# Two tiny reads ahead of the weight loads, and a DRAM copy cut into seven pieces, in a layernorm + S5 + SwiGLU kernel

## The chip, the cores and the metric

One core of a Trainium2 chip. The metric is the device time of one execution in microseconds, median of several runs. In the profile PE is TensorE's matmuls, PEld its weight loads, DVE VectorE, ACT ScalarE, POOL GpSimd and SP SyncE, which here only issues transfers. A q behind an engine's name means its instruction queue.

## What is computed

The input x is 2048 rows of 512, in bf16. It is normalised row by row, and the output is x plus an S5 state-space layer of the normalised rows plus a SwiGLU feed-forward layer of them. Cut to what matters:

```python
xn = (x - mean(x)) / sqrt(var(x) + 1e-5)                 # 2048 x 512
# A: S5 with 512 complex states
Bu = xn @ B_bar.T                                        # B_bar from Lambda, log_dt, B
h[t] = Lam_bar * h[t - 1] + Bu[t]
a = 2 * real(h @ C.T) + xn * Dskip
# B: SwiGLU
b = (silu(xn @ w_gate) * (xn @ w_up)) @ w_down           # 512 -> 1376 -> 512
out = x + a + b
```

w_gate and w_up are 512 x 1376 in bf16, so one row is 2,752 bytes and one matrix 1.4 MB.

## The kernel before

The 2048 rows are worked in four chunks of 512 (CW), each of four tiles of 128 rows (TPC); there are NT = 16 tiles. The inner size of 512 is four slices of 128, k = 0 to 3 (KD). The 1376 columns of gate and up are three groups (`fgroups`: columns 0 to 511, 512 to 1023, 1024 to 1279) and a rest of 96, loaded apart (`load_last`). The order of all work on every engine is written out by hand; an engine does its instructions in the order in which the program issues them.

**The head.** The first chunk is begun before any statistics are there. SyncE loads x tile 0 (L124) and ScalarE's queue x tile 1 (L127). Then the four k slices of gate group 0 are loaded in the loop at L129 and L130, through `load_w1_half` (L118): k = 0 and 2 from SyncE, k = 1 and 3 from ScalarE. SyncE goes on with x tile 2 (L131), the two halves of up group 0 (L132 and L133, again L118), x tile 3 (L134), groups 1 and 2 of gate and up (`load_w1`, L113), x tiles 4 to 7 (L143) and the transposing load of B's real part (L147). GpSimd loads three short rows of parameters (L142).

TensorE transposes x tiles 0 and 1 while taking the mean off (L251 and L259), DVE and ACT copy the result to SBUF (L263), and TensorE multiplies it with gate and up (`head_mm`, which calls `sw_mm`, L495): first gate with x tile 0, k = 0 to 3, then gate with x tile 1, then up with x tile 0, k = 0 to 3. Then comes the transpose of x tile 2, for which ACT takes the mean (L234) and DVE centres (L241); up with x tile 1; gate with x tile 2; the transpose of x tile 3; up with x tile 2; gate and up with x tile 3. The factor 1/std is put in when the products are taken out of PSUM (L504, L505). Groups 1 and 2 of the first chunk follow in the same way.

**The rest.** From about 24 us the chunks alternate: products with B (L393), with gate and up (L468), with w_down (L580) and with C (L590). DVE does the complex rotations and the scans (L435), ACT takes products out of PSUM.

**The output.** The output rows of tiles 0 to 11 start as a copy of x from DRAM to DRAM (L826), one transfer of 1.5 MB from SyncE, issued between the products with B of chunk 2 and the output of chunk 0. To it GpSimd's transfers add the results tile by tile (L597) and the skip term chunk by chunk (L564). Tiles 12 to 15 are written whole (L594).

Of the kernel before, what the change touches and what calls it, by code (L numbers as in the profile page):

```python
# [11 lines left out]
BF16 = mybir.dt.bfloat16  # L12
# [11 lines left out]
def kernel(  # L24
# [17 lines left out]
    nc = tc.nc  # L42
    _, L, D = A_x.shape
# [5 lines left out]
    NT = L // 128  # L49
    NCH = L // CW  # L50
    TPC = CW // 128
# [12 lines left out]
    const = ctx.enter_context(tc.tile_pool(name="const", bufs=1))  # L64
# [51 lines left out]
    def load_w1_half(q, tiles, view, gi, k0, k1):  # L116
        a, b = fgroups[gi]
        q.dma_start(out=tiles[gi][:, k0:k1, :], in_=view[:, k0:k1, a * 128:min(F, b * 128)])  # L118
# [7 lines left out]
    nc.vector.memset(minus_mean[:], -1.0 / D)  # L126
    nc.scalar.dma_start(out=xall[:, 1, :], in_=x_v[:, 1, :])  # L127
    nc.scalar.preload_act_table_set("silu_and_others")
    for k in range(KD):  # L129
        load_w1_half(nc.scalar if k % 2 else nc.sync, wg_g, wg_v, 0, k, k + 1)  # L130
    nc.sync.dma_start(out=xall[:, 2, :], in_=x_v[:, 2, :])  # L131
    load_w1_half(nc.sync, wu_g, wu_v, 0, 0, HK)  # L132
    load_w1_half(nc.sync, wu_g, wu_v, 0, HK, KD)  # L133
# [623 lines left out]
    def bproj_chunk(c):  # L757
        need(f"ln{c}")
        for part in range(2):
            for q in range(NQ):  # L760
                bproj_tile(c, part, q)
                pump(BP)
                multiply(0 if q else 1)
# [27 lines left out]
    def queue_ssm(c):  # L791
        fwd, back = ssm_ops(c)
        queue(f"ssm{c}", fwd + back)
# [29 lines left out]
    gateup_chunk(1)  # L823
    nc.gpsimd.dma_start(out=dsk_bc[:], in_=A_Dskip.partition_broadcast(128))
    bproj_chunk(2)
    nc.sync.dma_start(out=out[0, 0:(NT - TPC) * 128, :], in_=A_x[0, 0:(NT - TPC) * 128, :])  # L826
    queue_ssm(2)
    out_chunk(0)
    gateup_chunk(2)
# [45 lines left out]
```

## Time and profile before

| | |
|---|---|
| median of 3 runs | 179.22 us (179.06 to 179.39) |
| the profiled execution | 179.8 us |
| its span | 177.8 us |
| granted TensorE clock | 1.0 |
| DMA, mean over the span | 98 GB/s, 17.36 MB |

The span is the time from the first to the last instruction of the program in the profile; the execution's time has the start and the end around it as well. A group's line has the engine, the operation, output and inputs by the program's names, shapes and count. In a timeline line the first number is the start and the second the time from start to end of the merged instructions, in us; in brackets stands the idle time of the engine before it and what ended it. In a windows line stand, for each engine in the order PE, PEld, DVE, ACT, POOL, the busy time and the number of instructions, then the granted clock, the mean busy share of the 16 DMA engines and the GB/s that they moved. In a waits line the numbers are the total, the times and the longest wait, in us.

### The profile page before, as it was taken

How to read it: one execution, taken by the hardware profiler on the slowest of the kernel's cores; microseconds unless marked ns; L12 is line 12 of the kernel's file. 1: busy time of each engine (PE TensorE's matmuls, PEld its weight loads, DVE VectorE, ACT ScalarE, POOL GpSimd, SP SyncE). 2: the span in 40 equal slices, each digit the busy share in tenths (PEclk: the TensorE clock that was granted, in tenths of full speed). 3: DMA queues.
4: the chain of work that ended last, by engine and by line, in shares of the span. 5: the costliest groups of instructions: out<-in, count | busy, mean ns of one | idle time of the engine just before them, and what ended most of it. 6: DMA issues, size and time to landing. Idle time of an engine off the chain costs nothing.

```text
span 177.8 us, 2376 instructions
## 1 busy us (share of the span) xinstructions
PE 172.8 (97%) x856; PEld 82.5 (46%) x872; DVE 158.2 (89%) x261; ACT 109.0 (61%) x188; POOL 26.7 (15%) x36
## 2 busy tenths in 40 slices
PE   8899999999999999999999999999999999999993
PEld 5354664444444444444444444444444444444743
DVE  3799999999999999999999999999999997799033
ACT  4359989999977678036896661024866658863000
POOL 5162300050000000046000000025000002506100
PEclk9999999999999999999999999999999999999999
DMA  5999969999995000027123000008300001993612
GB/s 154 325 320 222 169 116 246 278 255 194 188 295 177 0 4 0 0 29 72 18 51 71 0 0 0 0 0 84 37 0 2 0 0 8 157 188 35 87 44 77
DMA packets 35115, 17.36 MB, mean 98 GB/s; under 512 B 24960, under 2 KB 35040, under 8 KB 35072
## 3 DMA queue, kind: packets, MB, share of 16 engines
q1 hardware_dynamic: 30928, 13.44, 32.6%
q0 software_dynamic: 3456, 3.28, 14.8%
q10 hardware_dynamic: 720, 0.49, 0.9%
q8 instruction: 7, 0.11, 0.3%
q14 instruction: 4, 0.03, 0.1%
HBM read 8.03 MB, written 5.24 MB: 75 GB/s over the span
## 4 chain that ended last, share of the span: by engine, by line
PE 94%; DMA 3%; issue 1%; SPq 0%; DVE 0%
PE ps L468 29%; PE ps L580 21%; PE ps L393 16%; PE ps L590 15%; PE ps L495 10%; DMA wg<-in_B_w_gate_dram 3%; PE ps L519 2%; PE ps L529 1%; PE ps L251 0%; SPq L118 0%; SPq L124 0%; DVE xall L593 0%; PE ps L287 0%
## 5 line engine op out<-in xcount | busy, mean ns | idle before, releaser
L580 PE MATMUL ps<-wd_sb,guT 128*128 128x512 bf16 (+4 forms) x195 | 38.6, 355 | 0.2
L468 PE MATMUL ps<-xnT,wg 128*128 128x512 bf16 x120 | 30.8, 379 | 0.1
L468 PE MATMUL ps<-xnT,wu 128*128 128x512 bf16 x114 | 30.0, 379 | 0.2
L435 DVE TENSOR_TENSOR_SCAN g<-r_t,car,u 128x512 bf16<-128x512 f32 x24 | 29.0, 1264 | 0.0
L393 PE MATMUL ps<-xnT,BT 128*128 128x512 bf16 x126 | 28.2, 379 | 0.2
L590 PE MATMUL ps<-CF,wt 128*128 128x512 bf16 (+2 forms) x140 | 28.1, 355 | 0.2
L580 PEld LDWEIGHTS <-guT 128*128 128x128 bf16 (+1 forms) x198 | 18.5, 98 | 19.9
L597 POOL DMA_DIRECT2D out_dram<-res x12 | 10.5, 1044 | 83.4 <-ACT res L596 77.5
L596 ACT CAST res<-ps 128x512 bf16<-128x512 f32 x12 | 7.0, 584 | 25.7 <-PE ps L590 23.4
L395 ACT CAST u<-ps 128x512 bf16<-128x512 f32 x32 | 17.9, 593 | 5.6 <-PE ps L393 5.5
L482 ACT ACTIVATE guT<-ps 128x512 bf16<-128x512 f32 x30 | 17.9, 596 | 5.1 <-PE ps L468 5.1
L483 ACT CAST u<-ps 128x512 bf16<-128x512 f32 x30 | 17.6, 586 | 5.1 <-PE ps L468 4.8
L590 PEld LDWEIGHTS <-wt 128*128 128x128 bf16 x144 | 13.5, 98 | 14.3
L393 PEld LDWEIGHTS <-BT 128*128 128x128 bf16 x128 | 12.5, 98 | 14.9
L468 PEld LDWEIGHTS <-wg 128*128 128x128 bf16 x120 | 11.6, 98 | 14.5 <-issue 0.8
L468 PEld LDWEIGHTS <-wu 128*128 128x128 bf16 x120 | 11.7, 98 | 14.2
L552 ACT ACTIVATE xr<-xall,nb,rstd 128x512 bf16<-128x512 bf16 x16 | 11.8, 804 | 4.3 <-DVE xall L560 2.5
L495 PEld LDWEIGHTS <-CF 128*128 128x128 bf16 x96 | 9.3, 99 | 8.9 <-ACT CF L263 1.8
L495 PE MATMUL ps<-wg,CF 128*128 128x512 bf16 (+1 forms) x48 | 11.1, 351 | 0.7 <-DMA wg<-in_B_w_gate_dram 0.7
L204 POOL TENSOR_TENSOR rstd<-ve,neg_half 128x1 f32<-128x1 f32 (+1 forms) x7 | 6.9, 988 | 27.0 <-DVE ve L203 27.0
L495 PE MATMUL ps<-wu,CF 128*128 128x512 bf16 (+1 forms) x47 | 10.6, 343 | 0.1
L194 DVE BATCH_NORM_STATS2 stats<-xall 128x6 f32<-128x512 bf16 x15 | 10.1, 672 | 0.0
(116 smaller groups left out, 200.7 us busy)
## 6 DMA issues: line engine op xcount, KB each, us to landing
out_dram<-in_A_x_dram SPq DMA_DIRECT2D x1, 1536.0 KB, 7.2
out_dram<-res POOLq DMA_DIRECT2D x12, 128.0 KB, 3.2
out_dram<-xall POOLq DMA_DIRECT2D x3, 512.0 KB, 6.6
wd_sb<-in_B_w_down_dram SPq DMA_DIRECT2D x1, 1280.0 KB, 6.8
xall<-in_A_x_dram SPq DMA_DIRECT2D x1, 1024.0 KB, 6.5
wu<-in_B_w_up_dram SPq DMA_DIRECT2D x3, 256.0 KB, 5.3
wg<-in_B_w_gate_dram SPq DMA_DIRECT2D x1, 512.0 KB, 6.1
wu<-in_B_w_up_dram SPq DMA_DIRECT2D x1, 512.0 KB, 4.9
```

Of the source, the lines that this page charges most:

```text
L194: nc.vector.bn_stats(out=stats[:, n, 0, :], in_=xall[:, n, :])
L393: nc.tensor.matmul(ps[:], lhsT=BT[:, part, k, q * 128:(q + 1) * 128], rhs=xnT[:, c, k, :], start=(k == 0), stop=(k == KD - 1))
L395: nc.scalar.copy(out=u_tiles[c][:, part, q, :], in_=ps[:])
L435: V.tensor_tensor_scan(out=g()[:, part, q, :], data0=r_t[:, q:q + 1].to_broadcast([128, CW]), data1=u_tiles[c][:, part, q, :], initial=ini ...
L468: nc.tensor.matmul(ps[:fs, lo:hi], lhsT=wslice(groups, fi, k), rhs=xnT[:, c, k, lo:hi], start=(k == 0), stop=(k == KD - 1))
L482: nc.scalar.activation(out=guT[:fs, fi, :], in_=psg[:fs], func=ACT.Silu)
L483: nc.scalar.copy(out=u_pair[c][:fs, fi % 2, :], in_=psu[:fs])
L495: nc.tensor.matmul(ps[:, 0:(b - a) * 128], lhsT=xcT[:, k, i * 128:(i + 1) * 128], rhs=groups[gi][:, k, :], start=(k == 0), stop=(k == KD - 1))
L552: nc.scalar.activation(out=box["xr"][:], in_=xall[:, n, :], func=ACT.Identity, scale=rstd[:, n:n + 1], bias=nb[:, n:n + 1])
L580: nc.tensor.matmul(o[:], lhsT=gu_tiles[c][:fsz[fi], fi, i * 128:(i + 1) * 128], rhs=wd_sb[:fsz[fi], fi, lo:hi], start=(fi == 0), stop=False)
L590: nc.tensor.matmul(o[:], lhsT=w_tiles[c][:, part, q, i * 128:(i + 1) * 128], rhs=CF[:, part, q, lo:hi], start=False, stop=(part == 1 and q ...
L597: nc.gpsimd.dma_start(out=out_v[:, n, lo:hi], in_=res[:, lo:hi], accum_op=ALU.add)
```

## The change

Two transfers are added on SyncE's queue, `touch(0)` ahead of the gate slices and `touch(1)` between them and x tile 2. Each reads the first two elements (4 bytes) of every 16th row of w_gate or w_up, 32 rows in all, into a small tile `touched` that nothing reads. The copy of x to the output, one transfer of 1536 rows, becomes seven: five of 256 rows and two of 128, one behind the other on the same queue.

```diff
     nc.scalar.preload_act_table_set("silu_and_others")
+    TB = 16
+    touched = const.tile([D // TB, 2, 2], BF16, name="touched")
+
+    def touch(part):
+        src = (B_w_gate, B_w_up)[part].rearrange("(a b) f -> a b f", b=TB)
+        nc.sync.dma_start(out=touched[:, part, :], in_=src[:, 0, 0:2])
+
+    touch(0)
     for k in range(KD):
         load_w1_half(nc.scalar if k % 2 else nc.sync, wg_g, wg_v, 0, k, k + 1)
+    touch(1)
     nc.sync.dma_start(out=xall[:, 2, :], in_=x_v[:, 2, :])
...
     bproj_chunk(2)
-    nc.sync.dma_start(out=out[0, 0:(NT - TPC) * 128, :], in_=A_x[0, 0:(NT - TPC) * 128, :])
+    cuts = [*range(0, NT - TPC - 1, 2), NT - TPC - 1, NT - TPC]
+    for a, b in zip(cuts, cuts[1:]):
+        nc.sync.dma_start(out=out[0, a * 128:b * 128, :], in_=A_x[0, a * 128:b * 128, :])
     queue_ssm(2)
```

## The prediction

> **What bounds the kernel now.** I read the share of busy time first, then the chain of waits, then the waits of TensorE and of the SyncE queue, then the first 12 us instruction by instruction, and last the DMA rate by window. From the page:
>
> ```profile
> PE 172.8 (97%) x856; PEld 82.5 (46%) x872; DVE 158.2 (89%) x261; ACT 109.0 (61%) x188; POOL 26.7 (15%) x36
> ...
> PE 94%; DMA 3%; issue 1%; SPq 0%; DVE 0%
> ```
>
> TensorE (PE) is the chain for 94% of the span; the only other share of weight is a gate load (DMA, 3%). The same chain in order of time, and TensorE's waits with their total:
>
> ```profile
> 1.66 4.99 DMA wg<-in_B_w_gate_dram
> 6.65 0.04 issue
> 6.69 2.36 PE ps L495 x10
> ```
>
> ```profile
> PE ps L647 <- PEq L859: 0.8, 1, 0.8
> PE ps L495 <- DMA wg<-in_B_w_gate_dram: 0.7, 1, 0.7
> ```
>
> After the start TensorE waits once in the whole kernel, for the gate slice k=2, issued by SyncE at 1.66 and landed at 6.65. From 6.69 to the end it runs without a gap, so the end moves by exactly what the stretch before 6.69 gives or takes, as long as no later input comes too late. The stretch itself, TensorE's timeline:
>
> ```profile
> 4.91 0.61 PE L495 MATMUL ps<-wg,CF 128*128 128x512 bf16 x1
> 5.31 0.42 PE L259 MATMUL ps<-diag,minus_mean 128*128 128x256 bf16 x1
> 5.52 0.51 PE L495 MATMUL ps<-wg,CF 128*128 128x512 bf16 x1
> 6.69 1.46 PE L495 MATMUL ps<-wg,CF 128*128 128x512 bf16 x6 [0.66 <-DMA wg<-in_B_w_gate_dram]
> 7.98 1.07 PE L495 MATMUL ps<-wu,CF 128*128 128x512 bf16 x4
> ```
>
> Matmuls of this shape start 0.216 us apart (1.03 us for four, the last one's 0.38 included). Without the wait the third would start at 5.52 + 0.22 = 5.74: the wait is worth 6.69 - 5.74 = 0.95 us. But 7.98 to 9.05 is 0.04 us longer than the other groups of four, because the second half of the up weights (issued 3.13, 5.3 us to landing, so 8.42) comes just when its matmul is due (8.46). Behind the gate slice stands a second bound at the same height: gate alone, made earlier, brings nothing; the up half must come earlier as well.
>
> Why these loads are slow: DMA share and GB/s are the last two columns.
>
> ```profile
> 2.00:3.00 1.00, 1.00 (x7) 0.62 (x5) 0.00 (x0) 0.60 (x1) 1.00 (x2) 1.00 0.98 320
> 3.00:4.00 1.00, 1.00 (x11) 0.80 (x10) 0.82 (x2) 0.53 (x1) 0.55 (x2) 1.00 0.95 238
> 4.00:5.00 1.00, 1.00 (x10) 0.78 (x9) 0.82 (x4) 0.53 (x4) 0.00 (x0) 1.00 0.98 244
> ...
> 7.00:8.00 1.00, 1.00 (x7) 0.41 (x6) 0.12 (x1) 0.72 (x2) 0.18 (x1) 1.00 1.09 386
> ...
> 28.00:29.00 1.00, 1.00 (x6) 0.48 (x5) 0.82 (x2) 1.00 (x3) 0.00 (x0) 1.00 0.61 86
> ...
> 30.00:31.00 1.00, 1.00 (x6) 0.42 (x5) 0.97 (x2) 1.00 (x3) 0.00 (x0) 1.00 1.04 364
> 36.70:37.70 1.00, 1.00 (x6) 0.42 (x5) 1.00 (x2) 1.00 (x3) 1.00 (x1) 1.00 0.86 186
> ...
> 39.70:40.70 1.00, 1.00 (x9) 0.37 (x8) 0.86 (x9) 0.84 (x2) 0.00 (x0) 1.00 1.08 385
> ```
>
> At 3 to 5 us, where the gate slices are read for the first time, 240 GB/s; at 7 to 8 us, where the other columns of the same rows are read, 386. The late x rows (from 27) and the down weights (from 36.7) show the same: slow for some 2 us at the start of a tensor, then full rate. In the packet records a 1,024-byte packet takes 46 ns as a rule, while in 3.0 to 6.6 us single ones take 400 to 1128 ns, and between 6.9 and 8.2 none takes over 180. That looks like a cost of reading a stretch of DRAM for the first time.
>
> **The change, part by part.** *Two touches.* Each is 32 reads of 4 bytes, 16 rows (44 KB) apart, two to each of 16 DMA engines. Issue: a SyncE transfer here takes 0.37 to 0.51 us and POOL's 4-row ones up to 0.71; I take 0.41, the gate slice's own, nearest in queue and kind. The first touch moves gate k=0 from 1.20 to 1.66 and k=2 from 1.66 to 2.12. k=0 landed at 3.80 and is used at 4.91, released by DVE's copy, so 1.1 us cover its delay. k=1 and k=3 go out on ScalarE's queue and don't move. The second touch goes out at about 2.6.
>
> *Waits that shift.* SP's and ACT's transfers take eight semaphores in turn by the trace's records, each issue waiting for the landing of the transfer eight earlier. The waits of SyncE's queue show it once:
>
> ```profile
> SPq L113 <- DMA wg<-in_B_w_gate_dram: 2.1, 1, 2.1
> ```
>
> That is the up load of group 1 waiting until 6.66 for gate k=2 (6.65). With two more transfers in the row x tile 2 must wait for x tile 0 (3.12), the up halves for x tile 1 (3.45) and the first touch, x tile 3 for a gate slice. So x tile 2 goes out at about 3.15 instead of 2.13, the halves at 3.6 and 4.15 instead of 2.60 and 3.13, x tile 3 at 4.6 instead of 3.59: each 1.0 us later. Group 1 of gate waits for gate k=2 in its turn: up to 6.65 instead of 4.10, landing at most about 12.7 instead of 10.18, used at 13.71 (12.76 with the full gain). What follows on that queue (up group 1, group 2, x tiles 4 to 7, the B transposes, the x transpose landing at 20.53 for a use at 24.27) has 1 us or more of cover, so up to about 1 us of delay costs nothing there.
>
> *What the touches may give.* Ahead of the end of the second up half each engine moves 88 packets (x tiles 0 to 2 and four gate slices, 8 each; two halves of 16): 88 x 0.046 = 4.05 us. First packet at 1.76, its first one 0.27 long, about 0.6 from last packet to landing (x tile 0): 1.76 + 0.27 + 4.05 + 0.6 = 6.7 without any long packet, against 8.42 measured. The late issue allows it: 4.15 + 1.0 to the first packet + 16 x 0.046 + 0.6 = 6.5. Full use of the 0.95 us asks for it at 7.46, so half of the long packets' time gone, (8.42 + 6.7) / 2 = 7.6, gives 0.8 us. A second condition: DVE's chain (mean of x tile 2 on ACT, centring, statistics of tile 3, centring at 9.86 to 10.21, used by TensorE at 10.84) begins with x tile 2 at 7.04 and has about 0.5 us to spare; a gain of 0.95 wants x tile 2 by 6.6. Bounds of the part: +0.95 gained if both come early, 0.5 if x tile 2 stays, and, with nothing warmed, up to 1.0 lost (the whole later issue shown in the up half). I take 0.75, between 0.5 and 0.95.
>
> *The copy in seven pieces.* Six more issues of 0.59 us: SyncE busy from 50.84 to about 55.0 instead of 51.4. It has nothing else until the x transpose at 91.33. The copy landed at 58.02, its first reader (the accumulating store) starts at 77.24: 19 us of cover. 2 + 6 is a full turn of eight, so from there on every wait has its old partner. Cost 0; without that cover it would be 6 x 0.59 = 3.5.
>
> *Does the end follow?* DVE is busy without a wait over 0.3 us from 28 to 142, so it cannot follow TensorE forward in that stretch; but its deliveries are early: rotated states of the last chunk done at 161.58 and read from 168.2, the scaled C at 71.74, read at 74.4, where 2.7 us is the least I found. 0.95 fits.
>
> *Sum.* The profiled execution took 179.8 us, of which 177.8 are its span and 2.0 lie around it; 177.8 - 0.75 = 177.05. It was 0.6 us above the median of the runs, 179.22, so I move the median: 179.22 - 0.75 = 178.5.
>
> The page DMA: Bandwidth & Descriptors of the Trainium skill (Latency and other measured facts) puts an HBM access at 0.2 us on average and 2 us at high load. By that rule the long packets come from load, and a touch cures nothing: the time would be 179.2 to 180.2. The trace speaks against it: 386 GB/s at 7 to 8 us with no long packet, 86 GB/s at 28 to 29 with many.
>
> **Rivals.** *The long packets stay and the touches hide* (0.15): they are due to load or rows of 2,752 bytes, or each engine must pay for itself and two rows warm little. The loads land as before, since the slow engine has a backlog: at 4.1 us about 180 of the first 768 packets have not started. For it: some packets of 200 to 750 ns at 8.3 to 10 us, in second reads. Against it: the clean stretch at 7 to 8. Time 179.2, within 0.35.
>
> *SyncE's queue becomes the bound* (0.30, slower): the touches warm too little, and x tile 2, the up halves and x tile 3 start 1.0 us later behind two issues and the shifted waits. It costs from the point where the up half lands after 8.42. For it: that half has 0 spare now. Against it: the backlog covers a part. Half shown: 0.5, whole: 1.0, so 179.7 to 180.2. Under this also falls that first reads are worked off one after the other: then gate gains what up loses.
>
> *The forecast* (0.55): 178.5, its own range 178.2 to 178.8.
>
> A difference under 0.2% (0.36 us) can't be told from no change here. The cases give faster 0.55, same 0.15, slower 0.30. Range: down to 178.1 (0.95 gained, and 0.17 of scatter as in the runs shown), up to 179.9, which leaves out the worse half of the slow case and little below.
>
> **What would show it.** Right: gate k=2 lands by 5.8 and the wait before the third matmul is gone; the second up half by 7.6, x tile 2 by 6.6; 3 to 5 us at over 300 GB/s; long packets few after 3.5 us. Wrong: gate early but TensorE then idle for `wu`, or for x tile 2; the up half after 8.42; the first matmul of L495 later than 4.91 because the touch itself holds up k=0. The copy is wrong if POOL's stores at 77 wait for it.

## The result, and the profile after

The changed kernel takes 179.72 us (median of 22 runs, 179.46 to 181.58), the kernel before 179.22 (22 runs, 178.77 to 179.76): slower, ratio 1.0032, interval 1.0018 to 1.0046, some 0.5 us. The forecast was 178.5. The profiled execution of the changed kernel took 179.73 us, its span is 177.8, the same as in the profile of before. So the two profiles don't show the loss; why is the first thing to be learned here.

New line numbers: L134 issues the touches, L140 loads x tile 2, L143 x tile 3, L504 is `sw_mm` (before L495), L260 and L268 are the transposes (before L251 and L259). The chain of waits of the changed kernel, its first 9 us:

```profile
0.74 2.35 DMA xall<-in_A_x_dram
3.09 0.02 issue
3.11 0.38 SPq L140
...
3.53 0.43 SPq L118
...
4.01 4.37 DMA wu<-in_B_w_up_dram
8.37 0.04 issue
8.42 0.59 PE ps L504 x2
```

Read from below: TensorE waited for the second up half (landed 8.37), which was issued at 4.01, because the first half and x tile 2 (3.11) stood ahead of it on SyncE's queue. In the chain of before the late load was gate k=2. SyncE's timeline:

```profile
0.74 0.39 SPq L124 DMA_DIRECT2D xall<-in_A_x_dram  x1
1.19 0.41 SPq L134 DMA_DIRECT2D touched<-in_B_w_gate_dram  x1
1.65 0.89 SPq L118 DMA_DIRECT2D wg<-in_B_w_gate_dram  x2
2.59 0.43 SPq L134 DMA_DIRECT2D touched<-in_B_w_up_dram  x1
3.11 0.38 SPq L140 DMA_DIRECT2D xall<-in_A_x_dram  x1
3.53 0.94 SPq L118 DMA_DIRECT2D wu<-in_B_w_up_dram  x2
```

In the kernel before, the same stretch of the queue was:

```profile
1.20 0.89 SPq L118 DMA_DIRECT2D wg<-in_B_w_gate_dram  x2
2.13 0.43 SPq L131 DMA_DIRECT2D xall<-in_A_x_dram  x1
2.60 0.95 SPq L118 DMA_DIRECT2D wu<-in_B_w_up_dram  x2
```

A touch costs 0.46 us of the queue (1.19 to 1.65), and x tile 2 and the up halves go out 0.9 to 1.0 us later than before (3.11, 3.53, 4.01 for 2.13, 2.60, 3.13). The turn of the semaphores adds little: SyncE is done with the second touch at 3.02, and x tile 2 waits from there until x tile 0 has landed (3.09). The DMA rate by window (DMA share and GB/s at the end):

```profile
3.00:4.00 1.00, 1.00 (x11) 0.79 (x10) 0.85 (x2) 0.53 (x1) 0.54 (x2) 1.00 0.70 135
4.00:5.00 1.00, 1.00 (x9) 0.75 (x8) 0.81 (x4) 0.56 (x4) 0.00 (x0) 1.00 0.91 285
7.00:8.00 1.00, 1.00 (x6) 0.48 (x5) 0.58 (x2) 0.39 (x2) 0.15 (x1) 1.00 0.90 274
```

No sign of warming: 135 GB/s from 3 to 4 us where it was 238, and 274 at 7 to 8 where it was 386. Between 3 and 8 us the records have 12 packets of 400 ns and more, up to 1032, where the kernel before has 9. The rates alone prove little, because less had been asked for by 4 us; experiments 3 and 7 test it.

**Where the time lies.** In 16 of the 17 profiles of this study, from the first matmul that transposes x tile 2 to the start of the last matmul, 166.00 to 166.01 us pass (166.04 in the other). So a span is the start of that transpose (the *head*), 166.0, 0.55 to the last result of VectorE, and a *tail* from there to the end. The profiles, in us:

| kernel | second up half issued, landed | head | tail |
|---|---|---|---|
| before | 3.13, 8.42 | 8.89 | 2.39 |
| changed | 4.01, 8.37 | 8.85 | 2.39 |
| changed, second profile | 4.00, 8.11 | 8.59 | 2.38 |
| four other profiles with the same loads at the start as before | 3.08 to 3.15, 7.38 to 8.06 | 7.88, 7.94, 8.24, 8.54 | by their transfers, below |

The profile that the forecast was made from has the slowest of five heads of the same code. Its execution, 179.8, was above all the runs known then; the median run has a span near 177.2, so a head near 8.3. In the changed kernel runs from 179.46 to 180.03 stand for heads of 8.5 to 9.1, and two runs (181.04 and 181.58) for something else.

### The profile page after: what moved, and what is told of

The parts are those of the page before. It is cut to its first block, busy times and chain, and to the rows that moved or that the text cites. A ratio compares the mean times of both kernels' runs of the same rounds, so it can differ in the third digit from the quotient of the medians.

```text
span 177.8 us, 2388 instructions
## 1 busy us (share of the span) xinstructions
PE 172.9 (97%) x856; PEld 82.5 (46%) x872; DVE 158.2 (89%) x261; ACT 109.1 (61%) x188; POOL 26.8 (15%) x36
## 4 chain that ended last, share of the span: by engine, by line
PE 93%; DMA 4%; issue 1%; SPq 0%; DVE 0%
PE ps L477 29%; PE ps L589 21%; PE ps L402 16%; PE ps L599 15%; PE ps L504 9%; DMA wu<-in_B_w_up_dram 2%; PE ps L528 2%; DMA xall<-in_A_x_dram 1%; PE ps L538 1%; PE ps L260 0%; SPq L118 0%; SPq L140 0%; DVE xall L602 0%; PE ps L296 0%
## 5 line engine op out<-in xcount | busy, mean ns | idle before, releaser
L504 PEld LDWEIGHTS <-CF 128*128 128x128 bf16 x96 | 9.3, 99 | 8.3 <-issue 0.9
L504 PE MATMUL ps<-wg,CF 128*128 128x512 bf16 (+1 forms) x48 | 10.9, 350 | 0.5 <-DVE CF L272 0.5
L504 PE MATMUL ps<-wu,CF 128*128 128x512 bf16 (+1 forms) x47 | 10.7, 343 | 0.2
```

The costliest lines, as they stand in the source:

```text
L504: nc.tensor.matmul(ps[:, 0:(b - a) * 128], lhsT=xcT[:, k, i * 128:(i + 1) * 128], rhs=groups[gi][:, k, :], start=(k == 0), stop=(k == KD - 1))
```

## The experiments

Theory P: the added transfers only send x tile 2 and the up halves out later, and the touches warm nothing. Rivals: D, the touches' own reads hold up the gate slices; C, the seven pieces cost something; F, the premise of the forecast, that first reads are slow and a touch cures it. The medians differ from session to session, so each stands beside that of before in the same session. Each kernel of the table has 6 to 12 runs. The ratio is taken over all of them and is not that of the two medians, so single long runs raise it (touches_only, gate_touch_8).

| kernel | median | before | ratio (interval) |
|---|---|---|---|
| pieces_only | 179.61 | 179.35 | 1.0014 (1.0000 to 1.0027) |
| touches_only | 180.19 | 179.35 | 1.0068 (1.0040 to 1.0096) |
| x_touches | 180.09 | 179.35 | 1.0043 (1.0030 to 1.0055) |
| pool_touches | 179.67 | 179.35 | 1.0017 (1.0003 to 1.0030) |
| after_again | 179.84 | 179.15 | 1.0041 (1.0025 to 1.0057) |
| x_touches_7 | 179.79 | 179.15 | 1.0033 (1.0021 to 1.0045) |
| late_touches_7 | 179.14 | 179.15 | 0.9997 (0.9980 to 1.0013) |
| tile2_on_act | 179.98 | 179.15 | 1.0042 (1.0025 to 1.0059) |
| copy_3 | 179.66 | 179.38 | 1.0019 (1.0003 to 1.0034) |
| gate_touch_8 | 179.68 | 179.38 | 1.0033 (1.0002 to 1.0064) |
| behind_gate_7 | 179.99 | 179.16 | 1.0040 (1.0026 to 1.0055) |
| up_touch_8 | 179.44 | 179.16 | 1.0011 (0.9998 to 1.0023) |
| after_dummies | 179.89 | 179.16 | 1.0036 (1.0024 to 1.0048) |

**1. The two parts apart.** The kernel before with the seven pieces alone:

```diff
-    nc.sync.dma_start(out=out[0, 0:(NT - TPC) * 128, :], in_=A_x[0, 0:(NT - TPC) * 128, :])
+    cuts = [*range(0, NT - TPC - 1, 2), NT - TPC - 1, NT - TPC]
+    for a, b in zip(cuts, cuts[1:]):
+        nc.sync.dma_start(out=out[0, a * 128:b * 128, :], in_=A_x[0, a * 128:b * 128, :])
```

> Only the copy in seven pieces, no touches. Theory P (the two added transfers on SyncE's queue send x tile 2, the up halves and x tile 3 out 0.9 us later) and theory D (the touches' own reads hold up the gate slices behind them in the queue) both expect no difference from before, within 0.2 us. Theory C (the seven pieces cost something, at the copy or behind it) expects the +0.5 us.

And the touches alone, with the copy whole (the first part of the diff of the change):

> Both touches on SyncE, the copy whole. P and D expect all of the loss, +0.5 us. Theory C expects 0. A difference from the changed kernel would mean that the turn of the semaphores behind the copy matters; none expected.

The pieces alone: 0.26 us, at the edge of what can be told; 0.13 of it is a longer tail. The touches alone lose more (0.84) than with the pieces (0.5 to 0.7), which no theory had foreseen. The profiles show why: the tail is 2.39 us before, 2.52 with six transfers added, 2.75 with two and 2.39 with eight. The kernel ends with waits of SyncE for its DMA semaphores in a fixed order, some 0.06 us each by the records. SP and ACT transfers take eight semaphores in turn; before, the last store, which lands last, has the semaphore that is waited for last. Two transfers more, and it has one of the first: six waits, 0.36 us, follow its landing (from its landing to the end 0.92 us pass in the kernel before and 1.29 with two more). So the seven pieces are worth about 0.36 us *beside the touches* (2 + 6 = 8).

**2. The tail by itself.** The kernel before with the copy in three pieces:

```diff
+    cuts = [0, 4, 8, 12]
```

> The kernel before with the copy in three pieces: two transfers added, 50 us into the kernel and with nothing waiting for them. If the tail goes by the number of added transfers modulo eight, it is 2.75 instead of 2.39 and the time +0.36 us (+0.2%). If only the head matters, 0.

Tail 2.76, time +0.28, ratio 1.0019: as expected. The two kernels of experiment 7 add ten and nine transfers, which is two and one beyond a full turn; their tails are 2.76 and 2.83, so six and seven waits follow the landing there too.

**3. Reads that warm nothing, in the same places.**

```diff
-        src = (B_w_gate, B_w_up)[part].rearrange("(a b) f -> a b f", b=TB)
-        nc.sync.dma_start(out=touched[:, part, :], in_=src[:, 0, 0:2])
+        src = A_x[0, 0:128, :].rearrange("(a b) f -> a b f", b=4)
+        nc.sync.dma_start(out=touched[:, part, :], in_=src[:, part, 0:2])
```

> Two transfers of the same shape in the same places, but they read 4 bytes of every 4th row of x tile 0, which the load ahead of them in the queue has just read: same issues, same shifted waits, no first read of gate or up. P expects +0.5 us or more (nothing is warmed, the delay stays). D expects 0 to +0.2 us, and gate k=0 landing by about 4.3 instead of 5.45.

With the copy whole: +0.74, of which the tail (2.76) is 0.37. Gate k=0 landed at 5.65, not at 4.3, though nothing of gate had been read ahead of it: against D, if D means the first reads of gate. The same with the copy in seven pieces, in one session with the changed kernel again:

> The changed kernel once more, on the same chip as the next three. From the profiles so far the span is made of three pieces: the start of the transpose of x tile 2 on TensorE (the head), 166.01 us from there to the last matmul, the same to 0.01 in seven profiles, and a tail from the last VectorE result to the end of the span that goes by the number of added SP and ACT transfers modulo eight: 2.39 us for 0, 2.75 for 2, 2.52 for 6. Eight are added here, so theory H (all of the loss is in the head) expects +0.4 to +0.6 us against before and a tail of 2.39.

> The two reads of x tile 0's rows in the touches' places, with the copy in seven pieces, so that the tail is 2.39 again. Theory P (the added issues delay what follows on SyncE's queue) expects the loss of the changed kernel, +0.4 to +0.6 us, and 0.3 to 0.4 less than the same reads with the whole copy (+0.75). If warming gave the touches something, this one is slower than the changed kernel by that much.

1.0041 and 1.0033, intervals that overlap widely: it makes no difference what the tiny transfers read. The touches warm nothing that can be measured.

**4. The same touches elsewhere.** Behind x tile 3, ahead of gate group 1:

```diff
-    touch(0)
     for k in range(KD):
...
-    touch(1)
...
     nc.sync.dma_start(out=xall[:, 3, :], in_=x_v[:, 3, :])
+    touch(0)
+    touch(1)
```

> Both touches behind x tile 3 instead of ahead of gate k=0 and x tile 2, copy in seven pieces: the head's loads go out as in the kernel before, at the same times. P expects no difference from before, within 0.2 us, gate k=0 landing at about 3.8 and a tail of 2.39. A loss of 0.4 or more would say that the reads themselves, or the turn of the semaphores, cost the time wherever they stand.

0.9997, gate k=0 at 3.75, tail 2.38: the loss is gone, while both transfers and all pieces are there. It is their place that costs. On GpSimd's queue instead:

```diff
-        nc.sync.dma_start(out=touched[:, part, :], in_=src[:, 0, 0:2])
+        nc.gpsimd.dma_start(out=touched[:, part, :], in_=src[:, 0, 0:2])
...
+    touch(0)
+    touch(1)
     ident = const.tile([128, 128], BF16, name="ident")
```

> Both touches as GpSimd's first work, on its own queue: SyncE's and ScalarE's queues and waits are as before, while the same first reads of gate and up are made, at about 1.5 to 2.5 us. P expects no loss, and if first reads are what slows the loads, a gain of 0.2 to 0.5 us. D expects a loss of some tenths again, with gate slices landing late.

A small loss, 0.3, where P expected none and F a gain. In its one profile the loads were early (gate k=0 at 3.75, second up half at 7.45) and TensorE waited for none, so D isn't seen here either. But its matmuls went to the faster pace only at 6.6 us, a matter taken up below:

```profile
4.91 0.61 PE L504 MATMUL ps<-wg,CF 128*128 128x512 bf16 x1
...
5.52 2.13 PE L504 MATMUL ps<-wg,CF 128*128 128x512 bf16 x7
7.49 1.03 PE L504 MATMUL ps<-wu,CF 128*128 128x512 bf16 x4
8.35 0.39 PE L260 MATMUL ps<-ident,CF 128*128 128x128 bf16 x4
```

One profile doesn't settle this 0.3; it stays open.

**5. Which of the late loads.** Both touches between the gate slices and x tile 2, so that gate goes out as before:

```diff
-    touch(0)
     for k in range(KD):
         load_w1_half(nc.scalar if k % 2 else nc.sync, wg_g, wg_v, 0, k, k + 1)
+    touch(0)
     touch(1)
```

> Both touches between the gate slices and x tile 2, copy in seven pieces: gate slices go out as in the kernel before, x tile 2 and the up halves 0.9 us later, as in the changed kernel. If the up halves carry the loss: +0.4 to +0.5 us, second half landing after 8. If gate k=0 carries it: 0 within 0.2 us. In both cases no run 1 us or more above the rest, because TensorE does not wait for gate k=0.

The whole loss and more than was expected (+0.83), with gate k=0 landing at 3.84. TensorE's timeline of this kernel:

```profile
4.77 0.39 PE L504 MATMUL ps<-wg,CF 128*128 128x512 bf16 x1
...
5.92 1.24 PE L504 MATMUL ps<-wg,CF 128*128 128x512 bf16 x5 [0.22 <-DMA wg<-in_B_w_gate_dram]
8.04 1.28 PE L504 MATMUL ps<-wu,CF 128*128 128x512 bf16 x4 [0.88 <-DMA wu<-in_B_w_up_dram]
9.15 0.38 PE L260 MATMUL ps<-ident,CF 128*128 128x128 bf16 x4
```

The wait has moved from gate to up: 0.88 us of idle time end with `wu`. One touch each, with the copy in eight pieces:

```diff
-    touch(0)
+    cuts = [0, 2, 4, 6, 8, 9, 10, 11, 12]
```

> The up touch alone, copy in eight pieces: gate slices as before, x tile 2 and the up halves 0.45 us later. If the up halves carry the loss: +0.15 to +0.3 us, like the gate touch alone without its long runs. If gate k=0 carries it: 0.

```diff
-    touch(1)
+    cuts = [0, 2, 4, 6, 8, 9, 10, 11, 12]
```

> The gate touch alone, and the copy in eight pieces (1 + 7 added, tail 2.39). Gate k=0 is late as in the changed kernel (lands after 5), the up halves go out 0.45 instead of 0.9 us later. If the up halves' issue decides, +0.2 to +0.3 us, half of the changed kernel's; if gate k=0 behind the touch decides, all of it, +0.5. Where TensorE waits long for gate k=0, some runs 1 to 2 us longer, because its matmuls then go on at 0.427 instead of 0.216 us apart for some us, as the profile of both touches with the whole copy shows.

Up alone +0.28 with no long run; gate alone +0.30, of which three long runs of twelve (181.2 to 181.6) make a part; the median of the other nine is 179.56, +0.18. Half the delay costs less than the whole, wherever it is put. Whether it is half can't be told: the interval of the up touch alone reaches down to no loss.

**6. Less delay than before.** x tile 2 issued from ScalarE's queue, so that the up halves leave earlier:

```diff
-    nc.sync.dma_start(out=xall[:, 2, :], in_=x_v[:, 2, :])
+    nc.scalar.dma_start(out=xall[:, 2, :], in_=x_v[:, 2, :])
```

> The kernel before with x tile 2's load issued from ScalarE's queue behind gate k=3, so that the two up halves and x tile 3 go out 0.47 us earlier from SyncE. If the issue time of the up halves bounds the head in the kernel before as well, a gain of 0.2 to 0.4 us; if in that kernel the DMA engines are behind with their work anyway, so that earlier issues bring nothing, 0 within 0.2 us, or a small loss where x tile 2 comes later.

A miss, by more than the small loss allowed for: +0.83. The chain of waits, with the line numbers of before:

```profile
3.11 5.24 DMA xall<-in_A_x_dram
...
8.44 0.73 ACT xnT L234 x2
...
9.19 0.36 DVE CF L241
...
9.60 0.40 PE ps L251 x4
```

x tile 2 left at 3.11, held by the turn of the semaphores until x tile 0 had landed, arrived at 8.35 and carried mean, centring and transpose with it. The up halves, issued at 2.12 and 2.60, landed at 7.21 and 8.06, no earlier than in most profiles of before. So in the kernel before, as far as this one profile shows, the halves are not bound by their issue, and earlier issue doesn't help; later issue hurts.

**7. Is a first read slow?** Extra reads in a quiet stretch of the kernel before, one after the other:

```diff
+    read(bx_v[0])
+    read(bx_v[0])
+    nc.sync.dma_start(out=probe[0:16, 0, 0:2], in_=B_x[0, 512:1024, :].rearrange("(a b) d -> a b d", b=32)[:, 0, 0:2])
+    read(bx_v[1])
+    read(bx_v[2])
+    read(bx_v[2])
+    read(bx_v[3])
```

> The kernel before, with ten extra reads from SyncE at a time when its queue and the DMA engines are idle (from about 95 us), one after the other, into a tile that nothing uses: x rows 0 to 511 again; B_x (an input that the kernel never reads) rows 0 to 511, first and second time; a touch (4 bytes every 32 KB) of rows 512 to 1023, then those rows; rows 1024 to 1535 first and second time; rows 1536 to 2047 first; gate group 0 twice. Theory F (a stretch of DRAM is slow when it is first read, and a touch takes that away): first reads 1 to 2 us longer than second ones, the touched one like a second one. If each DMA engine must pay for itself, the touched read is as long as a first one. Theory L (long packets come from load alone): all 512 KB reads of the same shape alike within 0.3 us.

One run, each read issued when the one before it had landed. By the records, from issue to landing: first 3.25, second 3.39; touched 3.36; first 3.19, second 3.21; first 3.42. The view of the last four of these, minimum, median and maximum:

```profile
DMA to landing us min/median/max: 3.2/3.3/3.4
```

With rows of 2,752 bytes:

```diff
+    rows = B_x[0].rearrange("s d -> (s d)")[0:640 * F].rearrange("(r f) -> r f", f=F)
```

> As the extra reads before, but shaped like the weight loads: B_x, which the kernel never reads, taken as rows of 2,752 bytes, and 1,024 bytes read of each. Rows 0 to 255 first time, second time, their next 1,024 bytes; a touch of every 16th of rows 256 to 511, those rows, again; rows 512 to 639 first and second time. Theory F (first reads of such rows are slow and a touch cures it): first reads longer than second by 0.5 us or more, the touched one not. If there is no such thing, all reads of one size alike within 0.3 us.

For rows 0 to 255 first, again, and their next columns, 256 KB each:

```profile
DMA to landing us min/median/max: 2.6/2.7/2.7
```

The touched rows took 2.61, again 2.68; 128 KB first 2.08 and again 2.09. F falls, for the patterns tried and with nothing else in flight. Long packets come in second reads too: the longest was 579 ns in the second read of the first rows, 312 in the first. The rival of the prediction that puts them down to rows of 2,752 bytes has a hint for it: 12 to 16 of the 256 packets of such a read took over 150 ns, first or second, against 2 to 8 of 512 with the plain rows. It was not followed up, and what stretches packets in the head, where three queues start at once, was not settled. (The read of x ahead of these overlapped a transposing load, the two gate reads the accumulating stores; they say nothing.)

**8. The long runs.** Single runs 1 to 2 us above the others came with the changed kernel (3 of 34), touches_only (2 of 7) and gate_touch_8 (3 of 12); none stood out so with before or any kernel whose gate k=0 is on time. TensorE's timeline in a long run, that of touches_only (181.66):

```profile
4.19 0.84 PE L268 MATMUL ps<-diag,minus_mean 128*128 128x128 bf16 x5
5.68 0.59 PE L504 MATMUL ps<-wg,CF 128*128 128x512 bf16 x1 [0.65 <-DMA wg<-in_B_w_gate_dram]
6.06 0.42 PE L268 MATMUL ps<-diag,minus_mean 128*128 128x256 bf16 x1
6.28 3.19 PE L504 MATMUL ps<-wg,CF 128*128 128x512 bf16 x7
```

Seven matmuls take 3.19 us, 0.427 apart; in the changed kernel's profile seven take 1.78. Here the pace changed to 0.216 only at 9.9 us, in the other profiles between 3.5 and 6.7, and the head was 10.38. The idle time filled with dummy matmuls:

```diff
+    dummy(warm, 6, 128)
     head_mm(0, 0, 0, 1)
```

> The changed kernel with six more dummy matmuls of 128 columns on TensorE, where it waits for gate k=0. If the idle time there is what now and then delays the switch to 0.216 us between matmuls, no run is 1 us or more above the others (3 of 34 of the changed kernel are), and the others are as before the edit, since the up half lands later than these matmuls need. If the switch is late for another reason, long runs stay.

No long run in 12 (179.46 to 180.24), the rest as expected. With 3 of 34, twelve runs without one come by chance one time in three, and the 18 runs with x rows in the touches' places, where TensorE waits as long, had none either: the cause fits and isn't shown. The page TensorE: Matmul & The Clock Gate of the Trainium skill (Part 1: The HAM clock gate) says that full speed comes after a window of some 3.4 us of sustained work and that the windows run freely, not from the kernel's start. That fits a late change by one window or more, and the scatter from 3.5 to 6.7 us. The granted clock in the rows stays at 1.00 throughout, from 4 to 10 us of this long run too; only the spacing shows it.

## Why the prediction was wrong, step by step

- **What bounds the kernel.** Right in kind: TensorE, with the start alone to be won or lost, and in 16 of 17 profiles the end follows the head to 0.01 us. The *size* was wrong twice. The 0.95 us wait for gate k=2 was taken from the slowest of five heads, and the gain was then taken off the median. At a median head of 8.3 in place of 8.89, some 0.6 of it weren't there to win; the earliest of the five is 7.88. And the third matmul was put at 5.74, as if the pace were 0.216 from 5.52 on. pool_touches has the same first two matmuls (4.91, 5.52) and waits for nothing, yet its third starts at 5.95 and its fourth at 6.37, and up begins at 7.49 for 7.98: with the pace changing as late as there, the wait was worth 0.49.
- **"A cost of reading a stretch of DRAM for the first time."** The step that failed. The slow windows are real, but first reads by themselves are no slower (experiment 7), and reads of something else cost the same as the touches (3). The gain term, 0.75, is 0. Two of the signs came or nearly came: gate k=2 landed at 5.90 (6.65 before; asked for by 5.8) and x tile 2 at 6.58 (7.04; by 6.6). But four heads without any touch have them at 5.50 to 6.09 and 6.06 to 6.68, so these were draws.
- **Issue and shifted waits.** Right as a mechanism: the touch at 0.46 of the queue, x tile 2 at 3.15 (3.11 measured) and the halves at 3.6 and 4.15 (3.53 and 4.01). x tile 3 was put at 4.6 and left at 5.46, held until gate k=0 had landed (5.45); it landed at 8.74 against 8.78, so that cost nothing. "Half shown: 0.5" is what came. The second half landed at 7.38 to 8.42 in six profiles with the head loads issued as before and at 8.11 to 8.68 in seven with both touches or their stand-ins: means 7.85 and 8.29, half of the 0.9. The rival that had 0.30 was the case.
- **Gate k=0** was allowed 1.1 us of cover. Issued 0.46 later, it lands some 1.5 to 1.85 later (at 5.29 to 5.65 in seven profiles), and the first matmul of L504 starts at 5.49. The prediction carried its 2.6 us to landing along, but a slice issued at 1.65 lands about as late with no touch ahead of it: k=2, issued there, landed at 5.20 to 6.65 in the ten profiles with gate's loads as before. In most runs the late k=0 is hidden behind the up half; it may be what opens the way to the long runs, which the prediction didn't have.
- **The copy.** 0 at its place, right (its pieces landed by 58.97). Missed was the end of the kernel: the full turn of eight was seen, but costed at nothing, where two without the six give 0.36.

## What to carry to other kernels

Ahead of loads that are needed at once, each extra transfer sends what stands behind it on the queue out later by its issue time, 0.46 us here, however little it moves. Two of them cost some 0.5 us of the whole; the same two behind those loads cost nothing that could be measured. Before building on a wait of some tenths, look at how much that wait scatters from run to run: one profile of a short, DMA-bound start is one draw. Test a cause by doing the same with the cause taken out (here: tiny reads of rows that another load was fetching anyway) before believing that it acts.

## What the runs showed of the hardware that was not expected

- The end of a kernel depends on which of eight DMA semaphores the last store gets: tails of 2.39, 2.52, 2.75 and 2.83 us for 0 or 8, 6, 2 and 9 added transfers.
- Reads of 512 KB alone took 3.2 to 3.4 us, whether first, second or touched; 256 KB in rows of 2,752 bytes 2.6 to 2.7.
- The change from 0.427 to 0.216 us between matmuls fell between 3.5 and 6.7 us in 16 profiles of nearly the same start, and once at 9.9.
